# More products of a constant tile on TensorE in the first attention units of a fused attention and gated feed-forward kernel

## The chip, the cores and the metric

One NeuronCore of a Trainium2 chip runs the whole program. The metric is the device time of one execution in microseconds (us), as the median of several runs. Runs of one kernel spread by about 0.3% here.

## The reference

Three stages are computed one after the other, all in float32 at the interface. The weights of the second stage arrive as 64-bit floats.

```python
def _attn_ref(q, k, v, n_sink, window):       # q, k, v: (4, 8, 768, 64)
    scores = scale * np.matmul(q, k.transpose(0, 1, 3, 2))
    keep = is_sink | in_window                # 4 sink columns, window of 128
    scores = np.where(keep, scores, -1000000000.0)
    a = np.exp(scores - max); a = a / (sum + 1e-09)
    return np.matmul(a, v)

def _moe_ref(x, w_gate, w_val, w_out):        # x: (3072, 512), d_ff 1536
    gate = 1.0 / (1.0 + np.exp(-(x @ w_gate)))
    return gate * (x @ w_val) @ w_out

def _moe2_ref(x, phi, w1, w2):                # 8 experts of 4 slots, soft routing
    d = softmax over tokens of (x @ phi); slot_input = d.T @ x
    slot_out[e] = np.maximum(slot_input[e] @ w1[e], 0.0) @ w2[e]
    return softmax over slots of (x @ phi) @ slot_out
```

## The kernel before

The tokens of the four batches are cut into eight half-sequences of 384 tokens. Each has four pairs of heads, and each pair has three units of 128 queries; so a half-sequence is units 0 to 11, the next 12 to 23, and so on.

A unit u of attention goes through pieces, which a list puts in a fixed order. `stage_a(u)` ("scores") multiplies queries and keys of the two heads on TensorE (PE, L301; each head fills 64 of the 128 rows), reduces the masked scores on VectorE (DVE, L305), takes the exponential on ScalarE (ACT, L322) and queues the normalisation (DVE L326 and L327, GpSimd or POOL L328). `stage_b(u)` ("transposes") transposes the probabilities on PE (L362 or L368) and copies them out of PSUM on ACT (L363, L375). It stands two units behind the scores. `stage_c(n)` ("values") multiplies by the values for a whole pair of heads (PE L393, L396) and copies the result into the rows `xh` that the next stage reads. It stands behind the transposes of the pair's third unit.

The feed-forward stage (`gemm1`, L633; `gemm2`, L671) works on a half-sequence in steps of two blocks of 128 hidden columns. A gate or value product of the first half-sequence is four full float32 products of 384 columns, one for each pair of heads (d = 0 to 3), summed in a PSUM tile of the tag `gv`. It can take its first three products before the last pair's values are there. The weights come from 64-bit floats by a chain of ACT (L514, L515), DVE (L518, L519, L522) and POOL (L526); DVE's three instructions of one weight block are called a conversion here.

Program order is: the pieces of attention until the first half-sequence's values are complete, and then the feed-forward steps with the other pieces between them. A scheduler that simulates a timeline then chooses each engine's final order, so steps of the feed-forward stage can stand among the attention pieces. PSUM tiles come from rings in program order: `gv` has three banks, `ys` (scores and second products) has three, `pt` and `xt` one each.

`warm_pe(k)` takes a `gv` tile and issues k products of a constant bf16 tile of zeros, `blank` (128 x 128 against 128 x 512, L267). They are called blanks here. Nobody reads their result. The blanks stay in program order on PE among the instructions that the scheduler places. In the kernel before, 12 stand at the beginning (L1009), and one ahead of the scores piece of each of the units 0 to 5.

Of the kernel before, what the change touches and what calls it, by code (L numbers as in the profile page):

```python
# [36 lines left out]
def fused_kernel(ctx, tc, qT, kA, kB, vB, vS, wg, wv, wo, phi, w1, w2, n_sink, window, out):  # L37
# [10 lines left out]
    def ps(tag, bufs, dt=F32):  # L48
        return psum.tile([128, 512], dt, name=tag, tag=tag, bufs=bufs)
# [213 lines left out]
    def warm_pe(k):  # L263

        t = ps("gv", 3)
        for _ in range(k):
            tc.keep_in_program_order(pe.matmul(t, blank[:, 0:128], blank, start=True, stop=True, skip_group_check=True))  # L267
# [154 lines left out]
    def attn_piece():  # L422
        if not pieces:
            return False
        f, u = pieces.popleft()
        emitted[0] += 1
        if f is stage_a and u < 6:
            warm_pe(1)
        f(u)
        if f is stage_c:  # L430
            c_done[0] += 1
            done_half[0] = c_done[0] // 4
        return True
# [184 lines left out]
    def gemm1(si, c, kind):  # L618
# [3 lines left out]
        if si == h_first[h] and c == 0 and kind == "g":  # L622
            while xs_n[0] <= x_order.index(h):
                while not x_can():
                    assert attn_piece()
                    tick()
                x_split()
# [378 lines left out]
    load_pair(0)  # L1006
    load_pair(1)
    pool.memset(blank, 0.0)
    warm_pe(12)  # L1009
    warm = per.tile([1, 1], F32, name="warm")  # L1010
    dve.memset(warm, 0.0)
    act.activation(out=warm, in_=warm, func=ACTF.Exp)
    with tc.tile_pool(name="setup", bufs=1) as cp:
        setup_masks(cp)
        attn_piece()
        attn_piece()
        for _ in range(3):
            w_load()
        sp.dma_start(out=phi_sb, in_=phi.rearrange("(k p) s -> p k s", p=128))
        setup_rest(cp)  # L1020
# [123 lines left out]
```

## Time and profile before

| | |
|---|---|
| median of 3 runs | 934.28 us (931.99 to 934.65) |
| the profiled execution | 932.42 us, span 930.6 us |
| PE busy | 893.3 us (96%) |
| DVE busy | 576.4 us (62%) |
| POOL, ACT busy | 475.6 us, 375.1 us |
| mean granted clock of PE | 0.971 |
| HBM | 116.62 MB read, 15.73 MB written |

The profile is of one execution. Busy time of PE counts from a product's start to a modelled end, so neighbouring products overlap in it. The granted clock is a share of 2.4 GHz: 1.00 is 2.4 GHz, 0.50 is 1.2 GHz. A half-sequence's attention runs alone until some 68 us; from there PE works on the feed-forward stage with attention between, and from some 740 us on the last half-sequence, the routing and the experts follow.

### The profile page before, as it was taken

To read this page: it belongs to the slowest core of one execution; us is meant where nothing else is said; L and a number is where in the kernel's file an instruction comes from. 1 tells how busy PE (TensorE), PEld (TensorE's weight loads), DVE (VectorE), ACT (ScalarE), POOL (GpSimd) and SP (SyncE) were. 2 spreads that over 40 slices of the span, in tenths; PEclk is the share of its full clock that TensorE was granted. 3 is DMA by queue.
4 is the path that set the end of the run, shared out by engine and by line. 5 is a ranking of instruction groups with operands and counts; after the bars stand their busy time and mean duration, and the time that the engine had idled before them with its cause. 6 is when DMAs were issued, how large, how long until landed. Compare 5 with 4: busy or idle time off the path is not lost. (4 is left out here: it accounts for less than half of the span.)

```text
span 930.6 us, 15349 instructions
## 1 busy us (share of the span) xinstructions
PE 893.3 (96%) x5277; PEld 712.4 (77%) x5277; DVE 576.4 (62%) x1620; ACT 375.1 (40%) x1000; POOL 475.6 (51%) x428
## 2 busy tenths in 40 slices
PE   8789999999999999999999999999999999899894
PEld 4445555567799999988889899898999997798453
DVE  7986769776566758765676667765555434444522
ACT  6775656443343344343443333443323223241221
POOL 4743436572566675665685746564545422684000
PEclk7789999999999999999999999999999999999897
DMA  7975557541222342322232323331222169656997
GB/s 234 309 249 170 206 163 263 172 112 46 80 72 76 92 112 64 89 80 83 64 113 73 98 77 103 83 87 51 72 57 68 47 235 387 225 157 193 306 332 237
DMA packets 80356, 133.41 MB, mean 143 GB/s; under 512 B 6800, under 2 KB 38544, under 8 KB 80272
## 3 DMA queue, kind: packets, MB, share of 16 engines
q1 hardware_dynamic: 80272, 132.37, 45.3%
q8 instruction: 43, 0.70, 0.3%
q14 instruction: 41, 0.34, 0.1%
HBM read 116.62 MB, written 15.73 MB: 142 GB/s over the span
## 5 line engine op out<-in xcount | busy, mean ns | idle before, releaser
L633 PE MATMUL gv<-xh,whv 128*128 128x384 f32 x432 | 151.0, 379 | 2.5 <-ACT whv L190 2.5
L633 PE MATMUL gv<-xh,whg 128*128 128x384 f32 x432 | 153.0, 383 | 0.0
L650 POOL TENSOR_TENSOR gl<-th,gh 128x384 fp32r<-128x384 f32 x84 | 88.6, 1055 | 117.1 <-DVE gh L192 95.9
L671 PE MATMUL ys<-who,gh 128*128 128x512 f32 x324 | 138.7, 455 | 1.5 <-DVE gh L192 1.5
L676 DVE SCALAR_TENSOR_TENSOR ysb<-ys,ysb 128x512 f32<-128x512 f32 x138 | 93.3, 685 | 38.9 <-PE ys L671 38.0
L633 PE MATMUL gv<-xh,wlv 128*128 128x384 f32 x336 | 114.6, 341 | 0.7 <-POOL wlv L496 0.7
L633 PE MATMUL gv<-xl,whv 128*128 128x384 f32 x336 | 114.1, 340 | 0.0
L633 PE MATMUL gv<-xl,whg 128*128 128x384 f32 x336 | 114.1, 340 | 0.0
L633 PE MATMUL gv<-xh,wlg 128*128 128x384 f32 x336 | 113.5, 338 | 0.0
L671 PE MATMUL ys<-wlo,gh 128*128 128x512 f32 x252 | 99.4, 395 | 0.0
L671 PE MATMUL ys<-who,gl 128*128 128x512 f32 x252 | 98.6, 396 | 0.0
L322 ACT ACTIVATE PC<-P,nb 128x132 f32<-128x132 f32 (+1 forms) x152 | 60.1, 396 | 91.2 <-DVE P L316 74.2
L328 POOL TENSOR_TENSOR PC<-PC,sm 128x264 f32<-128x264 f32 (+1 forms) x76 | 51.5, 677 | 88.5 <-DVE sm L297 61.4
L633 PEld LDWEIGHTS gv<-xh,whv 128*128 128x128 f32 x432 | 81.6, 190 | 18.3 <-issue 4.3
L633 PEld LDWEIGHTS gv<-xh,whg 128*128 128x128 f32 x432 | 81.4, 190 | 15.6 <-issue 4.9
L646 DVE SCALAR_TENSOR_TENSOR th<-th,gv 128x384 f32<-128x384 f32 x84 | 46.3, 551 | 69.7 <-PE gv L633 58.0
L496 POOL TENSOR_TENSOR wlv<-wraw,whv 128x512 fp32r<-128x512 f32 x48 | 63.6, 1326 | 47.6 <-ACT whv L190 39.2
L671 PEld LDWEIGHTS ys<-who,gh 128*128 128x128 f32 x324 | 59.7, 188 | 29.4 <-issue 18.2
L305 DVE CUSTOM_DVE_ANT_0 P<-ys,mask 128x260 f32<-128x260 f32 (+1 forms) x152 | 57.2, 392 | 39.3 <-PE ys L301 38.9
L496 POOL TENSOR_TENSOR wlg<-wraw,whg 128x512 fp32r<-128x512 f32 x48 | 62.9, 1310 | 31.8 <-ACT whg L190 28.7
L637 ACT ACTIVATE th<-gv 128x384 f32<-128x384 f32 x96 | 46.8, 488 | 80.2 <-PE gv L633 79.2
L496 POOL TENSOR_TENSOR wlo<-wraw,who 128x512 fp32r<-128x512 f32 x48 | 61.6, 1299 | 9.0 <-ACT who L190 7.0
(210 smaller groups left out, 1788.7 us busy)
## 6 DMA issues: line engine op xcount, KB each, us to landing
ew<-in_w_dram SPq DMA_DIRECT2D x32, 1024.0 KB, 12.0
wraw<-wsg SPq DMA_DIRECT2D x48, 256.0 KB, 2.7
wraw<-wsv SPq DMA_DIRECT2D x48, 256.0 KB, 2.6
wraw<-wso SPq DMA_DIRECT2D x48, 256.0 KB, 2.6
wbits<-in_wg_dram SPq DMA_DIRECT2D x12, 512.0 KB, 4.6
wbits<-in_wv_dram SPq DMA_DIRECT2D x12, 512.0 KB, 4.9
wbits<-in_wo_dram SPq DMA_DIRECT2D x12, 512.0 KB, 4.6
out_dram<-ew SPq DMA_DIRECT2D x8, 768.0 KB, 6.8
```

The source lines that it names most:

```text
L305: dve.tensor_tensor_reduce(out=P[:, h, 0:w], in0=S[:, 0:w], in1=mask[:, MOFF[mt]:MOFF[mt] + w], scale=-0.125, scalar=3.0e38, op0=ALU.add, ...
L322: act.activation(out=dst[:, h], in_=src[:, h], func=ACTF.Exp, scale=-1.0, bias=nb[:, h:h + 1], accum_out=sm2[:, h, 0:1])
L328: pool.tensor_tensor(dst, dst, sm.unsqueeze(2).to_broadcast([128, 2, src.shape[2]]), op=ALU.mult)
L496: pool.tensor_tensor(lo, r, hi.bitcast(F32), op=ALU.subtract)
L633: pe.matmul(acc_ps[:, 0:384], wt[:, 128 * d:128 * d + 128], xt[:, d, :], start=(k == 0), stop=(k == 4 * len(seq) - 1))
L637: act.activation(out=th, in_=acc_ps[:, 0:384], func=ACTF.Tanh, scale=0.5)
L646: dve.scalar_tensor_tensor(gr, th, 1.0, acc_ps[:, 0:384], op0=ALU.add, op1=ALU.mult)
L650: pool.tensor_tensor(gl, gr, gh.bitcast(F32), op=ALU.subtract)
L671: pe.matmul(yp, a[:, 128 * i:128 * i + 128], w, start=(k == 0), stop=(k == len(seq) * len(ns) - 1))
L676: dve.scalar_tensor_tensor(ysb[h][:, i, :], yp, 0.5, ysb[h][:, i, :], op0=ALU.mult, op1=ALU.add)
```

## The change

The blanks at the beginning are 24 in place of 12. The blanks among the pieces are three ahead of every scores piece and every transposes piece of the units 0 to 14, in place of one ahead of the scores pieces of the units 0 to 5. That is 114 in place of 18.

```diff
         f, u = pieces.popleft()
         emitted[0] += 1
-        if f is stage_a and u < 6:
-            warm_pe(1)
+
+        if f is not stage_c and u < 15:
+            warm_pe(3)
         f(u)
...
     pool.memset(blank, 0.0)
-    warm_pe(12)
+    warm_pe(24)
```

The edit moves other instructions too, since the scheduler places them anew. Lines behind L427 are one higher in the changed kernel (L633 is L634 there, L518, L519 and L522 are L519, L520 and L523).

On PE, around the transpose of pair 1's sink columns (`Tb`), the kernel before has this (`gv_724`, `gv_742`, `gv_799` are the first gate, the first value and the second gate product of the first half-sequence):

```order
L301 MATMUL ys_631<-rk_432,rq_431 128x260
L362 MATMUL pt_476<-ident_61,PW_391 128x128 x4
L372 MATMUL xt_483<-identr_62,Tb_128 128x128
L633 MATMUL gv_724<-xh_420,whg_348 128x384
L633 MATMUL gv_742<-xh_420,whv_373 128x384
L633 MATMUL gv_799<-xh_420,whg_794 128x384
L301 MATMUL ys_632<-rk_432,rq_431 128x260
```

and the changed kernel this, with the repeated rows of each three blanks left out:

```order
L267 MATMUL gv_460<-blank_137 128x512
...
L267 MATMUL gv_469<-blank_137 128x512
...
L267 MATMUL gv_496<-blank_137 128x512
...
L372 MATMUL xt_539<-identr_62,Tb_128 128x128
...
L267 MATMUL gv_507<-blank_137 128x512
...
L267 MATMUL gv_528<-blank_137 128x512
...
L362 MATMUL pt_532<-ident_61,PW_427 128x128 x4
```

The three product steps of d = 0 are gone from this place, and fifteen blanks stand around the transpose. The steps of d = 1 and d = 2 of the same three products, which stand behind pairs 2 and 3 in the kernel before, are gone from their places likewise.

On PE, where the first half-sequence's values end (L396 of pair 3) and the first gate product gets its fourth step, the kernel before has:

```order
L396 MATMUL xt_695<-ttb_130,vs_332 128x256
L362 MATMUL pt_731<-ident_61,PW_626 128x128 x4
L301 MATMUL ys_870<-rk_527,rq_526 128x260
L301 MATMUL ys_871<-rk_527,rq_526 128x260
L633 MATMUL gv_724<-xh_420,whg_348 128x384
L633 MATMUL gv_742<-xh_420,whv_373 128x384
L633 MATMUL gv_799<-xh_420,whg_794 128x384
L301 MATMUL ys_963<-rk_622,rq_621 128x260
```

and the changed kernel (`gv_832`, `gv_854` and `gv_915` are the same three products):

```order
L634 MATMUL gv_832<-xh_456,whg_376 128x384 x3
...
L396 MATMUL xt_803<-ttb_130,vs_356 128x256
...
L301 MATMUL ys_991<-rk_595,rq_594 128x260
L634 MATMUL gv_832<-xh_456,whg_376 128x384
...
L267 MATMUL gv_839<-blank_137 128x512
L634 MATMUL gv_854<-xh_456,whv_403 128x384 x4
...
L267 MATMUL gv_891<-blank_137 128x512
L634 MATMUL gv_915<-xh_456,whg_910 128x384 x4
...
L267 MATMUL gv_950<-blank_137 128x512
```

Of the nine steps that the kernel before has done by then, the changed one has the first product's three, just ahead; the other two products come whole behind it, and nine blanks stand between.

On DVE, between the score reductions (L305) of unit 14 and unit 15, the kernel before has:

```order
L305 ISA PW_678,nb_679<-ys_684,mask_125 128x260
L305 ISA nb_679 128x1
L522 SCALAR_TENSOR_TENSOR wA_1073<-wbits_1045,wA_1073 128x512
L326 TENSOR_REDUCE sm_681<-sm2_680 128x2
L305 ISA PW_756,nb_757<-ys_761,mask_125 128x260
```

and the changed kernel:

```order
L305 ISA PW_786,nb_787<-ys_792,mask_125 128x260
...
L519 TENSOR_SCALAR wA_1231<-wA_1231 128x512
L520 TENSOR_SCALAR wA_1231<-wA_1231 128x512
L523 SCALAR_TENSOR_TENSOR wA_1231<-wbits_1200,wA_1231 128x512
L326 TENSOR_REDUCE sm_789<-sm2_788 128x2
...
L519 TENSOR_SCALAR wA_1289<-wA_1289 128x512
L340 CAST Ta_127<-PC_717 128x12x4
L520 TENSOR_SCALAR wA_1289<-wA_1289 128x512
L341 TENSOR_TENSOR Ta_127<-PC_717,Ta_127 128x12x4
L523 SCALAR_TENSOR_TENSOR wA_1289<-wbits_1251,wA_1289 128x512
L305 ISA PW_868,nb_869<-ys_873,mask_125 128x260
```

Two whole conversions stand there now in place of the last instruction of one. Ahead of unit 14 twelve conversions and two instructions of the thirteenth stand in the kernel before, and thirteen in the changed one.

## Rows read from the trace of the kernel before

**Rows 1.** Busy time by stretch; the columns are named in the first row.
```profile
core 0: us, PE busy (x) PEld busy (x) DVE busy (x) ACT busy (x) POOL busy (x), PEclk, DMA share, GB/s
8.83:60.27 51.44, 40.78 (x185) 24.27 (x185) 46.04 (x153) 38.56 (x114) 30.63 (x26) 0.73 0.86 284
...
68.02:140.00 71.98, 71.98 (x302) 40.28 (x300) 50.24 (x133) 42.06 (x109) 29.14 (x24) 1.00 0.55 180
...
200.00:740.00 540.00, 540.00 (x3300) 477.20 (x3301) 341.17 (x973) 205.10 (x571) 310.77 (x280) 1.00 0.27 78
740.00:930.60 190.60, 166.74 (x1169) 129.21 (x1167) 77.08 (x169) 50.41 (x105) 61.58 (x52) 0.94 0.78 256
```

**Rows 2.** Waits of PE, 66 to 760 us: total, times, longest.
```profile
PE ys L301 <- DVE nb L305: 0.5, 1, 0.5
```

**Rows 3.** Timeline of PE at the start: start, duration, what.
```profile
1.31 5.66 PE L267 MATMUL gv<-blank 128*128 128x512 bf16 x13 [1.31 <-POOL blank L1008]
6.90 0.49 PE L301 MATMUL ys<-rk,rq 64*128 64x128 f32 x4
```

**Rows 4.** Timeline of PE, one-pass products of 512 columns in a stream.
```profile
739.28 0.39 PE L671 MATMUL ys<-who,gh 128*128 128x512 f32 x1
739.51 0.39 PE L671 MATMUL ys<-wlo,gh 128*128 128x512 f32 x1
739.74 0.40 PE L671 MATMUL ys<-who,gl 128*128 128x512 f32 x1
```

**Rows 5.** Busy time by stretch of one clock level, first half-sequence.
```profile
10.20:20.40 10.20, 9.69 (x33) 6.49 (x34) 7.64 (x44) 8.99 (x29) 4.49 (x4) 0.50 0.75 238
20.40:23.80 3.40, 2.28 (x13) 1.29 (x11) 3.40 (x12) 2.74 (x9) 2.67 (x3) 1.00 0.83 270
23.80:34.00 10.20, 7.19 (x35) 4.77 (x35) 10.06 (x38) 7.98 (x25) 7.18 (x7) 0.50 0.99 329
...
37.50:40.90 3.40, 3.40 (x6) 1.46 (x5) 3.37 (x6) 2.23 (x5) 2.62 (x4) 0.50 0.88 281
...
47.70:51.10 3.40, 3.40 (x6) 1.19 (x5) 2.06 (x9) 3.31 (x8) 0.99 (x2) 0.50 0.87 298
51.10:61.40 10.30, 7.67 (x52) 4.59 (x51) 9.21 (x21) 6.41 (x18) 5.84 (x5) 1.00 0.79 274
```

**Rows 6.** Timeline of PE, steps of the gate and value products.
```profile
37.31 1.45 PE L633 MATMUL gv<-xh,whg 128*128 128x384 f32 x2
...
67.27 0.91 PE L633 MATMUL gv<-xh,whg 128*128 128x384 f32 x2
...
70.59 2.79 PE L633 MATMUL gv<-xh,whv 128*128 128x384 f32 x8
```

**Rows 7.** Waits of DVE, 8.83 to 60.27 us.
```profile
DVE PW L305 <- PE ys L301: 2.1, 2, 1.6
DVE PW L305 <- PE pt L362: 1.0, 1, 1.0
DVE wA L518 <- ACT wA L514: 1.0, 1, 1.0
DVE P L305 <- PE ys L301: 0.5, 1, 0.5
```

**Rows 8.** Timeline of DVE: first reductions of units 0, 14, 16, and a mask step.
```profile
8.83 0.28 DVE L305 CUSTOM_DVE_ANT_0 P<-ys,mask 128x128 f32<-128x128 f32 x1
...
9.25 0.56 DVE L99 TENSOR_SCALAR mask<-mask 128x780 f32<-128x780 f32 x1
...
60.27 0.41 DVE L305 CUSTOM_DVE_ANT_0 PW<-ys,mask 128x260 f32<-128x260 f32 x1
...
66.15 0.43 DVE L305 CUSTOM_DVE_ANT_0 PW<-ys,mask 128x260 f32<-128x260 f32 x1
```

**Rows 9.** Groups of DVE instructions, 8.83 to 60.27 us: the conversions.
```profile
L518 DVE TENSOR_SCALAR wA<-wA 128x512 f32<-128x512 f32 x13 | 10.1, 774 | 1.0 <-ACT wA L514 1.0
L519 DVE TENSOR_SCALAR wA<-wA 128x512 int32<-128x512 int32 x13 | 9.9, 760 | 0.3
L522 DVE SCALAR_TENSOR_TENSOR wA<-wbits,wA 128x512 int32<-128x512 int32 x12 | 9.7, 808 | 0.2
```

## The prediction, made before the changed kernel ran

> **What bounds the kernel now.** I read the table of busy time by stretch first [rows 1]. It shows three regimes. From 68 us to 740 us TensorE (PE) is busy without a gap at a granted clock of 1.00, and from 66 to 760 us the list of waits holds a single one of PE, 0.5 us long [rows 2]. Whatever PE work is still undone when that stretch begins therefore moves the end. After 740 us PE is busy 166.74 of 190.6 us; I take that tail to move as a whole, since it starts from PE's last products. Before 68 us, attention of the first half-sequence fills the time: PE is busy 40.78 of 51.44 us between 8.83 and 60.27, DVE 46.04 of 51.44, at a mean PE clock of 0.73.
>
> Then I read that early part by clock level [rows 5]. The clock is 0.50 (1.2 GHz) in four stretches between 10.2 and 51.1 us, 27.2 us in all. In the first of these PE was busy 9.69 of 10.20 us, mostly with scores, which fill 64 of 128 rows. The clock there follows what PE works on, not only whether it works: between 51.1 and 61.4 us it stayed at 1.00 with PE busy 7.67 of 10.30 us. The 13 products at the start also ran at the low level although the clock column reads 1.00 there: 5.66 us for 13 is 435 ns each [rows 3], while a 512-column one-pass product late in the kernel follows its predecessor by 0.23 to 0.24 us [rows 4]. I price a blank product at 0.235 us at 2.4 GHz and 0.435 at 1.2 GHz. The Trainium skill (TensorE: Matmul & The Clock Gate, "Back-to-back issue gap") gives 216 ns for an isolated 512-column product at full clock; by it the blanks behind the first half would cost 0.2 us less, and no row here shows a blank in a stream at that level.
>
> Last I read DVE. It is idle 5.4 us between its first score reduction at 8.83 and that of unit 14 at 60.27 [rows 1, 8]; 3.6 us of that are waits for PE and 1.0 for ACT [rows 7]. Its work there is 46.04 us, of which some 30 are conversions of 64-bit weights [rows 9]. So the first half is DVE's stretch, with PE second.
>
> **The change part by part.** There are 24 blanks at the start and 30 pieces with three each, 114 in place of 18.
>
> The first 24: 13 run as before, to 6.97 us, and by then the stream has raised the clock, since the scores behind it run at the higher level (two of 128 columns begin at 6.90 and are through in 0.49 us [rows 3]). Ahead of those scores stand 27 now (24 and the first piece's three), so 14 more, 14 x 0.235 = 3.3 us: the first scores begin near 10.2 us. DVE read them at 8.83 before. In the new DVE order the 0.56 us mask step of L99 [rows 8] and four smaller steps stand ahead of that read, so most of the delay is covered. I charge 0.4 us; without that cover it is 1.4.
>
> The blanks inside the first half: by PE's order 105 of the 114 stand ahead of the first complete gate product, 27 of them ahead of the first scores, so 78 fall into the attention stretch, 78 x 0.235 = 18.3 us. What room is there? PE idles 10.66 us between 8.83 and 60.27 [rows 1]. In the four slow stretches it is busy 9.69 + 7.19 + 3.40 + 3.40 = 23.7 us [rows 5]; at 2.4 GHz half of that, 11.8 us, comes back. And nine one-column-block steps of the gate and value products, which filled holes there (the first three at 37.31 [rows 6]), leave the stretch: 9 x 0.70 = 6.3, with 0.70 from eight records in 2.79 us [rows 6]. Room 28.8 us, need 18.3: it fits if the clock stays up, and it does not if it falls: at 1.2 GHz the same blanks are 34 us and the 11.8 do not come back. I take the upper level for nearly all of it, because a stream of blanks alone raised the clock at the start.
>
> What that gives DVE: its waits for PE, 3.6 us, can go. Against that stand 0.8 us (by the new DVE order one third of a weight conversion more is done ahead of unit 14, a third of 774 + 760 + 808 ns [rows 9]), the 0.4 from above, and waits of the new order: scores now stand behind up to nine blanks and wait for one of three PSUM banks that DVE frees, so a late score is followed by a late blank. The trace has no row for that; it is between nothing and the 3.6 us that DVE waited for PE. I take 0.9. Unit 14: 8.83 + 46.04 + 0.8 + (5.4 - 3.6 + 0.4 + 0.9) = 58.8 against 60.27, so 1.5 us earlier. The ends are 55.7 (DVE never waits), 4.6 us earlier, and 2 us later.
>
> From unit 14 to unit 16: before, DVE came to unit 16's first reduction at 66.15, 5.9 us later, with less than one conversion between [rows 8]. Now two whole conversions, 2 x 2.34 = 4.7 us, stand between units 14 and 15; with the four score reductions, the norm and the two small steps it is 7.1 us: 1.2 us later. The scores that need those banks stand on PE ahead of the first full-depth step, so PE waits for it. With unit 14 earlier by 1.5, the first full-depth step ends 0.3 us earlier in sum.
>
> What is late next: the nine product steps that ran in holes. By the new order three of them stand just before that point and six do not run before it: the two other accumulators are now requested after the blanks' tiles in the same ring of three banks. That is 6 x 0.70 = 4.2 us of PE work carried into the stretch without gaps. The last nine blanks (units 12 to 14, transposes) stand in that stretch too: 9 x 0.235 = 2.1 us. Together 6.3 us, with nothing to hide it [rows 1, 2].
>
> Later PE order is the same from about 200 us on. The SP queue moves its weight loads and a value load ahead of two of the q/k loads; these are needed units later, so I cost that at nothing; the 1.0 us wait for ACT [rows 7] is what such loads cost at their worst before.
>
> Sum: -0.3 + 6.3 = +6.0 us. The profiled execution took 932.42 us (930.6 span plus 1.8 around it), so 938.4 by it; the median of the runs is 934.28, 1.86 above it, so 940.3 by that. I forecast 940.
>
> **A rule weighed.** The stretch from 68 to 140 us shows PE busy throughout, yet weight loads are busy only 40.28 of 71.98 us, against 477.20 of 540 between 200 and 740 [rows 1]. The Trainium skill (Trainium Kernel Development and Optimization, "Performance Expectations") says that busy time of matmuls is a bad measure of how near PE is to its limit and that the share of weight loads is a good one. By it PE would still have room until 140 us and part of the 6.3 us would vanish; with half of it gone the sum is that of the first rival below. The rows speak against: the eight records in 2.79 us are four full fp32 products of 384 columns with no gap between [rows 6], and such products hold the array long for each weight load.
>
> **Rivals.**
> No change: the carried work is half absorbed between 68 and 200 us, where DVE is the other busy engine. Then -0.3 + 3.1 = +2.8, 937.1; or DVE never waits, -4.6 + 1.2 + 6.3 = +2.9, 937.2. For it: PE's busy time has modelled ends. Against: only one wait of PE is listed.
> Faster: attention was held by the slow clock, DVE loses all 5.4 us of its idle time, and PE absorbs all the carried work after 68 us. -4.6 + 1.2 = -3.4, 930.9. It decides only if the stretch after 68 us has 6 us of room.
> Much slower: the clock does not stay up, because blanks are split into threes with scores and waits between. PE's load between 8.83 and 60.27 at 2.4 GHz would be 51.4 - 28.8 - 0.9 (four old blanks) + 18.3 = 40.0 us; with half of it at 1.2 GHz it is 60 us, PE becomes the bound and unit 14 comes 8.6 us later instead of 1.5 earlier: 934.3 + 8.6 + 1.2 + 6.3 = 950. It decides from the point where over 29% of that work runs slow (40.0 x 1.29 = 51.4).
> That the blanks do nothing for the clock is the same case: the old rate, 27.2 slow of 51.4 us, is about the half that I priced.
>
> **How the numbers follow.** Forecast (937.5 to 945): 0.54. No change: 0.23. Faster: 0.10. Slow clock: 0.13. A measurement of this kernel can tell about 0.3%, 2.8 us, from no change. Faster 0.10; within 0.3% 0.22 (nearly all of the no-change case); slower 0.68. The range leaves out the faster case and the far part of the slow-clock case: 934 to 948; the likeliest case's own is 937.5 to 945.
>
> **What would show it.** Right: granted clock near 1.00 from about 7 to 66 us with at most one or two short drops; blanks 0.235 us apart; DVE waits for PE under 2 us before unit 14; nine blanks and the second and third accumulators' first steps behind the first complete gate product; that product ending at 67 to 68 us; PE without gaps behind it and every later landmark about 6 us later. Wrong: that product ending before 62 us, PE gaps between 68 and 200 us, or long stretches at 0.50 with blanks 0.43 us apart.

## The result, and the profile after

The changed kernel takes 943.58 us (median of 4 runs, 942.95 to 944.04), the kernel before 934.46 (4 runs, 931.99 to 935.05). The ratio is 1.0112 with a 95% interval of 1.0089 to 1.0136: slower by 9.1 us. Forecast was 940, with a range of 934 to 948. The profiled execution took 944.04 us (span 942.2), so the two profiles shown are 11.6 us apart, of which 10.4 are there by 740 us.

**Stretches.** Busy time by stretch of the changed kernel, with the columns of [rows 1]:

```profile
8.83:63.58 54.75, 49.59 (x250) 26.43 (x248) 48.78 (x154) 39.99 (x115) 29.60 (x26) 0.84 0.84 276
10.73:63.58 52.85, 47.69 (x240) 25.62 (x239) 47.04 (x149) 39.99 (x115) 29.60 (x26) 0.84 0.83 271
15.80:22.60 6.80, 6.50 (x18) 3.17 (x18) 6.42 (x21) 4.98 (x16) 4.24 (x4) 0.50 0.86 273
22.60:29.50 6.90, 5.95 (x34) 3.55 (x32) 6.37 (x33) 6.25 (x18) 5.26 (x6) 0.99 0.97 321
29.50:39.70 10.20, 9.56 (x42) 5.61 (x42) 8.31 (x29) 7.76 (x29) 5.72 (x6) 0.50 0.88 295
39.70:63.58 23.88, 21.48 (x136) 11.53 (x133) 21.34 (x52) 16.21 (x41) 12.74 (x11) 1.00 0.73 236
72.12:140.00 67.88, 67.88 (x284) 37.09 (x283) 41.62 (x111) 38.49 (x99) 26.24 (x23) 1.00 0.48 159
200.00:740.00 540.00, 539.80 (x3303) 475.36 (x3301) 345.59 (x983) 206.17 (x577) 314.72 (x283) 1.00 0.28 80
```

Two stretches of the first half are left at 0.50, 17.0 us together, where [rows 5] show four of 27.2. PE's mean clock up to unit 14 rose from 0.73 to 0.84, and its busy share from 79% to 91%. The wait list of PE from 66 to 760 us again holds a single wait, so the long stretch has no gap here either:

```profile
PE ys L672 <- DVE nb L305: 1.0, 1, 1.0
```

**Start.** Timeline of PE (start, duration, what), which answers to [rows 3]:

```profile
1.31 8.08 PE L267 MATMUL gv<-blank 128*128 128x512 bf16 x27 [1.31 <-POOL blank L1009]
9.32 0.49 PE L301 MATMUL ys<-rk,rq 64*128 64x128 f32 x4
9.75 0.82 PE L267 MATMUL gv<-blank 128*128 128x512 bf16 x3
```

The first scores come at 9.32, not at 10.2, and three blanks are through in 0.82 us: at the upper level the blanks are about 0.22 us apart.

**Landmarks.** Timeline of DVE: the first reductions of units 0, 14 and 16 [rows 8], and of two later units, 54 and 95:

```profile
10.73 0.28 DVE L305 CUSTOM_DVE_ANT_0 P<-ys,mask 128x128 f32<-128x128 f32 x1
...
63.58 0.42 DVE L305 CUSTOM_DVE_ANT_0 PW<-ys,mask 128x260 f32<-128x260 f32 x1
...
70.24 0.43 DVE L305 CUSTOM_DVE_ANT_0 PW<-ys,mask 128x260 f32<-128x260 f32 x1 [0.66 <-PE pt L362]
...
355.45 0.29 DVE L305 CUSTOM_DVE_ANT_0 P<-ys,mask 128x128 f32<-128x128 f32 x1 [1.67 <-PE ys L301]
...
733.04 0.43 DVE L305 CUSTOM_DVE_ANT_0 P<-ys,mask 128x260 f32<-128x260 f32 x1 [1.76 <-PE ys L301]
```

The same two late units in the kernel before:

```profile
345.01 0.29 DVE L305 CUSTOM_DVE_ANT_0 P<-ys,mask 128x128 f32<-128x128 f32 x1 [1.47 <-PE ys L301]
...
722.60 0.43 DVE L305 CUSTOM_DVE_ANT_0 P<-ys,mask 128x260 f32<-128x260 f32 x1 [1.76 <-PE ys L301]
```

Unit 0 is 1.9 us late, unit 14 3.3, unit 16 4.1, units 54 and 95 both 10.4. So 4.1 us are lost while attention runs alone, 6.3 us between unit 16 and unit 54, and nothing from there to 740.

**The first complete gate product.** Timeline of PE:

```profile
64.06 0.70 PE L301 MATMUL ys<-rk,rq 64*128 64x260 f32 x2 [1.25 <-DVE nb L305]
64.70 2.20 PE L634 MATMUL gv<-xh,whg 128*128 128x384 f32 x6
...
69.60 0.60 PE L362 MATMUL pt<-ident,PW 128*128 128x128 f32 x4
...
71.37 0.91 PE L634 MATMUL gv<-xh,whg 128*128 128x384 f32 x2
72.12 0.81 PE L267 MATMUL gv<-blank 128*128 128x512 bf16 x3
72.76 2.74 PE L634 MATMUL gv<-xh,whv 128*128 128x384 f32 x8
...
76.62 0.81 PE L267 MATMUL gv<-blank 128*128 128x512 bf16 x3
77.27 2.74 PE L634 MATMUL gv<-xh,whg 128*128 128x384 f32 x8
...
80.53 0.82 PE L267 MATMUL gv<-blank 128*128 128x512 bf16 x3
```

The first product has its three early steps just ahead (six records at 64.70), the next two come whole behind it (eight records each), and nine blanks stand between, as the order said.

**DVE.** Its waits from 8.83 to 63.58 us (total, times, longest) and its conversions, which answer to [rows 7, 9]:

```profile
DVE wA L519 <- POOL who L527: 1.5, 1, 1.5
DVE PW L305 <- PE pt L362: 1.2, 1, 1.2
DVE wA L519 <- ACT wA L515: 1.0, 3, 0.4
DVE xh L192 <- PE xt L396: 0.6, 1, 0.6
DVE P L305 <- PE ys L301: 0.5, 1, 0.5
DVE PW L305 <- PE ys L301: 0.4, 1, 0.4
```

```profile
L519 DVE TENSOR_SCALAR wA<-wA 128x512 f32<-128x512 f32 x13 | 11.7, 899 | 2.5 <-POOL who L527 1.5 <-ACT wA L515 1.0
L523 DVE SCALAR_TENSOR_TENSOR wA<-wbits,wA 128x512 int32<-128x512 int32 x13 | 10.6, 814 | 0.1
L520 DVE TENSOR_SCALAR wA<-wA 128x512 int32<-128x512 int32 x13 | 9.4, 720 | 0.3
```

The waits for PE shrank only from 3.6 to 2.7 us, and waits in the conversion chain (for POOL and ACT) grew from 1.0 to 2.5.

### The profile page after: what moved, and what is told of

Same layout as the page of the kernel before. It is cut to its first block, busy times and chain, and to the rows that moved or that the text cites. A ratio compares the mean times of both kernels' runs of the same rounds, so it can differ in the third digit from the quotient of the medians.

```text
span 942.2 us, 15531 instructions
## 1 busy us (share of the span) xinstructions
PE 910.1 (97%) x5373; PEld 715.8 (76%) x5373; DVE 578.8 (61%) x1620; ACT 375.5 (40%) x1000; POOL 473.0 (50%) x428
## 4 chain that ended last, share of the span: by engine, by line
## 5 line engine op out<-in xcount | busy, mean ns | idle before, releaser
L634 PE MATMUL gv<-xh,whg 128*128 128x384 f32 x432 | 151.3, 379 | 0.0
L634 PE MATMUL gv<-xh,whv 128*128 128x384 f32 x432 | 150.5, 376 | 0.5 <-ACT whv L190 0.5
L634 PE MATMUL gv<-xh,wlv 128*128 128x384 f32 x336 | 114.3, 340 | 0.7 <-POOL wlv L497 0.7
L634 PE MATMUL gv<-xl,whg 128*128 128x384 f32 x336 | 114.6, 341 | 0.0
L634 PE MATMUL gv<-xh,wlg 128*128 128x384 f32 x336 | 113.8, 339 | 0.1
L634 PE MATMUL gv<-xl,whv 128*128 128x384 f32 x336 | 113.8, 339 | 0.0
L634 PEld LDWEIGHTS gv<-xh,whg 128*128 128x128 f32 x432 | 80.4, 188 | 15.0 <-issue 4.2
L634 PEld LDWEIGHTS gv<-xh,whv 128*128 128x128 f32 x432 | 80.5, 189 | 13.9 <-issue 3.0
L305 DVE CUSTOM_DVE_ANT_0 P<-ys,mask 128x260 f32<-128x260 f32 (+1 forms) x152 | 56.9, 393 | 39.3 <-PE ys L301 39.0
## 6 DMA issues: line engine op xcount, KB each, us to landing
ew<-in_w_dram SPq DMA_DIRECT2D x32, 1024.0 KB, 12.2
```

The costliest lines, as they stand in the source:

```text
L305: dve.tensor_tensor_reduce(out=P[:, h, 0:w], in0=S[:, 0:w], in1=mask[:, MOFF[mt]:MOFF[mt] + w], scale=-0.125, scalar=3.0e38, op0=ALU.add, ...
L634: pe.matmul(acc_ps[:, 0:384], wt[:, 128 * d:128 * d + 128], xt[:, d, :], start=(k == 0), stop=(k == 4 * len(seq) - 1))
```

## The experiments

Twelve kernels ran. The table has the time against the kernel before on the same chip. Its other columns come from each profile, from 1.31 us to the first reduction of unit 54: PE's idle time; the blanks (for each the time from its start to the next product's start, or to its own end where that comes first); and the rest, which is PE's own products with what the low clock adds to them. The three add up to the column "unit 54" less 1.31. A profile is of one execution: those of e2 and e5 are 2.9 us faster than their kernels' medians. Up to four blanks have no record in those of e1, e2, e4 and e12, which moves a column by less than 1 us.

| kernel | median us | ratio (95%) | unit 14 | unit 54 | blanks | idle | rest |
|---|---|---|---|---|---|---|---|
| before | 932.67 to 934.46 | | 60.27 | 345.01 | 7.9 | 12.1 | 323.6 |
| changed | 943.58 | 1.0112 (1.0089 to 1.0136) | 63.58 | 355.45 | 29.5 | 7.0 | 317.6 |
| e1 units 0 to 5 only | 935.72 | 1.0027 (1.0016 to 1.0039) | 62.40 | 346.81 | 18.3 | 8.7 | 318.5 |
| e2 no nine late blanks | 942.75 | 1.0109 (1.0089 to 1.0129) | 62.00 | 352.53 | 27.1 | 7.4 | 316.7 |
| e3 64 columns | 942.91 | 1.0102 (1.0086 to 1.0119) | 63.60 | 355.64 | 13.2 | 10.5 | 330.7 |
| e4 one in place of three | 939.52 | 1.0076 (1.0055 to 1.0098) | 55.30 | 350.79 | 16.1 | 12.8 | 320.6 |
| e5 one blank in all | 932.14 | 0.9990 (0.9972 to 1.0007) | 58.05 | 341.72 | 0.6 | 13.2 | 326.6 |
| e6 12 at the start, no others | 929.25 | 0.9950 (0.9930 to 0.9969) | 54.95 | 340.19 | 4.5 | 12.4 | 322.0 |
| e7 24 at the start, then as before | 933.29 | 0.9997 (0.9986 to 1.0008) | 62.34 | 344.32 | 9.2 | 10.9 | 322.9 |
| e8 12 at the start, then as changed | 939.23 | 1.0056 (1.0038 to 1.0073) | 57.88 | 350.45 | 26.0 | 9.1 | 314.0 |
| e9 one PSUM tile for all blanks | 947.48 | 1.0157 (1.0131 to 1.0182) | 65.70 | 359.62 | 28.7 | 9.4 | 320.3 |
| e10 256 columns | 937.49 | 1.0049 (1.0034 to 1.0065) | 57.17 | 349.37 | 20.5 | 8.0 | 319.6 |
| e11 before, 12 more late | 934.10 | 1.0011 (0.9998 to 1.0024) | 60.16 | 345.72 | 10.5 | 12.2 | 321.7 |
| e12 before, 48 more late | 945.22 | 1.0126 (1.0104 to 1.0147) | 59.51 | 349.61 | 11.2 | 12.9 | 324.2 |

Only the first 24 of e12's 48 stand ahead of unit 54.

What the low clock adds can be estimated and taken out of the rest: half of PE's busy time on its own products in the stretches at 0.50. That is 12.8 us before, 5.9 in the changed kernel, 17.5 in e3, 10.5 in e6, 2.3 in e8, and 14.6 in e5 (the last section says why its clock column shows almost none of it). What is left is 309 to 314 us in all fourteen kernels. So PE's own work to unit 54 hardly changes, and the times differ by blanks, idle time and the low clock.

**e1, blanks in the first six units only**

```diff
-        if f is not stage_c and u < 15:
+        if f is not stage_c and u < 6:
```

> Three blanks ahead of the scores and transposes pieces of units 0 to 5 only, 24 at the start: 60 blanks. In the new order all nine early product steps stand ahead of the first complete gate product again and no blank behind it; the conversions on VectorE are as in the changed kernel up to unit 12, and 13 stand ahead of unit 14, 14 ahead of unit 16 (before 13 and a third, changed 15). Backlog theory (six steps and nine late blanks, 6.3 us, added behind the first complete gate product): every later landmark moves by no more than that product does, so the 6.3 us are gone. Conversion theory (attention is late by the conversions that the new order puts ahead of unit 16): product late by about 0.5 x 2.3 = 1 us, total 935.5. Blank-time theory (the blanks' own run time on TensorE delays attention): 33 of the 78 blanks of the stretch are left, so unit 14 late by 0.42 x 3.3 = 1.4 us, total 936. If the backlog theory is wrong: over 940.

Measured 935.72, 2.5 us over before, and unit 16 and unit 54 late by 1.5 and 1.8: nothing is added behind unit 16. That fits the backlog theory, and 935.5 or 936 doesn't part the other two. (In the table its blanks are 10.4 us more than before, idle time 3.4 and the rest 5.1 less.)

**e2, the changed kernel without its nine late blanks**

```diff
-        if f is not stage_c and u < 15:
+        if (f is stage_a and u < 15) or (f not in (stage_a, stage_c) and u < 12):
```

> As the changed kernel, without the blanks ahead of the transposes of units 12 to 14, nine of 114. These nine stood behind the first complete gate product; without them the ring of three banks frees earlier in program order too, and the new order has all nine early product steps ahead of that product. Conversions as in the changed kernel: 13 ahead of unit 14, 15 ahead of unit 16. Backlog theory: first complete gate product as in the changed kernel (72.1 us, 4.1 later than before), nothing added behind it: every later landmark +4, total 938.5. Without the backlog theory (only blank time counts): the nine blanks are worth 2.1 us, total 941.5.

A miss: 942.75, not 938.5; the other theory's 941.5 is nearer. The timeline of PE shows where the early steps went:

```profile
62.48 0.70 PE L301 MATMUL ys<-rk,rq 64*128 64x260 f32 x2 [1.25 <-DVE nb L305]
63.12 2.20 PE L634 MATMUL gv<-xh,whg 128*128 128x384 f32 x6
65.25 0.70 PE L301 MATMUL ys<-rk,rq 64*128 64x260 f32 x2
65.88 1.56 PE L634 MATMUL gv<-xh,whv 128*128 128x384 f32 x4
...
69.14 2.10 PE L634 MATMUL gv<-xh,whg 128*128 128x384 f32 x6
...
73.78 0.91 PE L634 MATMUL gv<-xh,whg 128*128 128x384 f32 x2
```

and DVE's first reduction of unit 16:

```profile
73.25 0.43 DVE L305 CUSTOM_DVE_ANT_0 PW<-ys,mask 128x260 f32<-128x260 f32 x1 [3.36 <-PE pt L362]
```

All nine steps (18 records) stand ahead of the first complete gate product again, but in no hole: PE has no gap from 62.48 until behind the last of them, and DVE waits 3.36 us for the transpose behind them. Unit 16 is 7.1 us late in place of 4.1, and little is added later. Which side of that product a step stands on decides only where the lateness shows. This led to the budget theory: until some 350 us the time is PE's products, plus blanks, plus idle time, plus the low clock's loss.

**e3, narrow blanks**

```diff
-            tc.keep_in_program_order(pe.matmul(t, blank[:, 0:128], blank, start=True, ...
+            tc.keep_in_program_order(pe.matmul(t[:, 0:w], blank[:, 0:128], blank[:, 0:w], start=True, ...
```

(w is 64 among the pieces and 512 at the start.)

> As the changed kernel, but the blanks among the pieces are 64 columns wide in place of 512 (the 24 at the start stay); 13 conversions ahead of unit 14 and 15 ahead of unit 16, as in the changed kernel; early product steps as in the changed kernel. Blank-time theory: unit 14's first reduction falls back to 60 us or earlier (63.58 changed, 60.27 before), first complete gate product near 68, then 4.2 for six steps and 0.5 for nine narrow blanks: 939. Conversion theory: unit 14 near 63 and the product near 72 in spite of the narrow blanks, total 943. The granted clock tells besides whether narrow blanks hold it as wide ones do (0.84 mean from 10.7 to 63.6 us in the changed kernel, 0.73 before).

Unit 14 at 63.60 and 942.91 us are the conversion theory's numbers, but not by its way. The stretch up to unit 14:

```profile
10.73:63.60 52.87, 44.34 (x241) 28.57 (x242) 44.75 (x150) 38.95 (x116) 29.99 (x26) 0.58 0.82 266
```

DVE was idle 8.1 us of it (5.8 in the changed kernel), and the clock fell to 0.58, below the 0.73 of the kernel before. Blanks fell by 16.3 us, the rest rose by 13.1 and idle time by 3.5: the same total. So the wide blanks do hold the clock better than narrow ones, and they cost what that gives back.

**e4, one in place of three**

```diff
-            warm_pe(3)
+            warm_pe(1)
```

> As the changed kernel, but one blank ahead of every such piece in place of three (24 at the start stay): 54 in all. By the new order the six steps stay behind the first complete gate product and three late blanks with them: backlog 4.2 + 0.7 = 4.9. Ahead of unit 14 stand only 11 conversions, ahead of unit 16 13 (before 13 and a third and 13 and two thirds; changed 13 and 15). Conversion theory: unit 14 at about 56 to 58, the product at 67 to 68, total 934.5 - 0.5 + 4.9 = 939. Blank-time theory: a third of the delay, 1.4, total 934.5 + 1.4 + 4.9 = 941.

Unit 14 comes at 55.30, earlier than the conversion theory's 56 to 58, and the total of 939.5 is that theory's 939, but not by its way. Unit 16 is 3.9 us early and unit 54 5.8 late: 9.7 us appear between them where 4.9 were expected. PE idles 2.9 us there (0.5 before), and the clock is at 0.50 from 170.6 to 174.0, which costs 1.7. When DVE reaches unit 14 does not set the end. The mean clock from 10.70 to 55.30 is 0.85, no lower than the 0.84 of the changed kernel: with one blank per piece it was held as well as with three.

**e5 and e6, none among the pieces**

```diff
-        if f is not stage_c and u < 15:
-            warm_pe(3)
         f(u)
...
-    warm_pe(24)
+    warm_pe(1)      # e5; 12 in e6
```

> One blank in all, at the start, none among the pieces. VectorE's conversions stand as before (13, 12 and 12 parts ahead of unit 14, 14, 13 and 13 ahead of unit 16), and the nine early product steps too. Budget theory (new, from the first four runs: until some 300 us TensorE's time is its own work, some 312 us, plus the blanks' time, plus its idle time, plus what the low clock costs, and the sum of the last three was 32.8 us before, 42.4 in the changed kernel): blanks fall from 7.9 to about 0.4 us; if nothing else moves, 7.5 us faster, 926; if blanks are what holds the clock, the loss by the low clock rises from 12.8 towards 20 and the total stays within 2 us of 933. Order theory (the time is set by when VectorE reaches units 14 and 16): no change, 933 to 934, and unit 14's first reduction at 60 to 61 us.

> 12 blanks at the start, none among the pieces (before has six there). Ahead of unit 14 stand 11 conversions, ahead of unit 16 13 (before 12.7 and 13.3). Budget theory: 6 x 0.235 = 1.4 us less of blanks, and less or more by what the six do for the clock: 930 to 934. Order theory: unit 14 at 56 to 57 us, unit 16 at 65, total 932 to 933.

e5 cannot be told from before (0.9990, runs from 929.3 to 936.2): 7.3 us of blanks less, rest and idle 4.1 more in its profile. The budget's 926 is out; its other case (within 2 us of 933) and the order theory's total are not told apart, though unit 14 at 58.05 is earlier than the order theory's 60 to 61. e6 is the fastest of all, 929.25, with the whole interval of its ratio at least 0.3% below 1. Against before, its blanks are some 3.5 us less, idle 0.3 more and the rest 1.6 less. Its first reduction of unit 54, at 340.19, comes 4.8 us earlier than that of before. The order theory's 932 to 933 is missed by 3, the budget's 930 to 934 by 0.8. Without the six blanks among its pieces, and with the order that the scheduler then finds, the kernel before is 0.5% faster.

**e7 and e8, the two halves of the edit**

```diff
-        if f is not stage_c and u < 15:
-            warm_pe(3)
+        if f is stage_a and u < 6:
+            warm_pe(1)      # e7: 24 at the start stay
...
-    warm_pe(24)
+    warm_pe(12)             # e8: three per piece stay
```

> 24 blanks at the start, among the pieces as before (one ahead of the scores of units 0 to 5). Budget theory: 12 x 0.235 = 2.8 us more of TensorE time ahead of the first scores (at 9.3 us against 6.9), paid back only as far as TensorE's idle time falls: 934 to 936.5. Order theory: 14 conversions ahead of unit 14 and 14.7 ahead of unit 16, one and a third and one more than before: unit 14 at 62 to 63 us, total +2 to +3, 936. Cover theory of the prediction (VectorE's other work hides the later start): 933.5 to 934.

> 12 blanks at the start, three ahead of every scores and transposes piece of units 0 to 14 as in the changed kernel. Six steps and nine late blanks stay behind the first complete gate product. Budget theory: 2.6 us of blanks less than the changed kernel, 940 to 941. Cover theory: as the changed kernel, 942.5 to 943.5.

24 at the start alone make no difference (933.29 against 933.75), though unit 14 is 2.1 us late. That is nearest the cover theory's 933.5 to 934; the budget's 934 to 936.5 is missed by 0.7, the order theory's 936 by 2.7. The pieces' blanks alone make 5.5 us of the 9.1: 939.23, near the budget's 940 to 941 and 3.3 below the cover theory's range. The halves don't add up: 12 more at the start cost nothing beside the old pieces, and 3.6 us (9.1 less 5.5) beside the new ones, where the rest is 3.6 us higher (317.6 against 314.0). e8 was at 0.50 for less time, a loss of 2.3 us against 5.9. Why the longer start brings the low clock back is open.

**e9, one bank for all blanks**

```diff
-        t = ps("gv", 3)
+        if not blank_t:
+            blank_t.append(ps("gv", 3))
+        t = blank_t[0]
```

> All 114 blanks of the changed kernel, but all write one PSUM tile of the tag gv that is taken once, so that two of the three banks are free for the gate and value products from the start. By the new order the first two accumulators' three early steps each stand among the attention pieces again (six steps), and the third product whole behind the first complete gate product, with nine late blanks. 15 conversions stand ahead of unit 14 and of unit 16. Carried-steps theory (of the prediction: the six steps are lost because the blanks hold the ring): the three steps of one more accumulator and more come back, total 940 to 941. Budget theory (TensorE's time until some 300 us is its own work plus blanks, idle and the low clock's loss, wherever a step stands): blanks take their 29.5 us as in the changed kernel, idle plus low clock at 11 to 13 us as there: 942 to 945.

947.48, the slowest of all. Giving six early steps their banks back did not bring their 4.2 us back. It is also above the budget's 942 to 945, by 2.5 us: idle time and the low clock's loss are 15.6 us in place of 11 to 13. Between units 16 and 54 PE idles 3.6 us (1.3 in the changed kernel), and the clock is at 0.50 from 199.2 to 202.6, which costs 1.6. Why the new order waits there is open.

**e10, half as wide**

```diff
-            warm_pe(3)
+            warm_pe(3, 256)
```

> As the changed kernel, but the 90 blanks among the pieces are 256 columns wide in place of 512 (64 in the narrow kernel); the 24 at the start stay 512 wide. 11 conversions stand ahead of unit 14, 13 ahead of unit 16. Budget theory: blanks 8.1 us for the first 27 and some 10 us for the others, 18 in sum. If the clock holds as with wide blanks (loss by the low clock 6 us, idle 8): sum 32, 933 to 935. If it falls as with narrow ones (loss 17.5, idle 10.5): sum 46, over 945. Order theory: unit 14 at 56 us, and 4.2 for six steps and 1 for nine late blanks: 936 to 938.

937.49, between the two cases of the budget: blanks 9.0 us less than in the changed kernel, idle and rest 3.0 more. The half-width blanks hold the clock less well: its mean is 0.78 from 10.59 to 57.17 us, between the 0.84 of the changed kernel and the 0.73 before, and the loss is 6.7 us against 5.9. The order theory's 936 to 938 fits too, though unit 14 at 57.17 is followed by unit 54 4.4 us late.

**e11 and e12, more blanks where nothing is idle**

```diff
         if f is stage_a and u < 6:
             warm_pe(1)
+        if f is stage_a and u == 40:                  # e11
+        if f is stage_a and u in (40, 52, 64, 76):    # e12
+            warm_pe(12)
```

> The kernel before with twelve more blanks in one place, ahead of the scores piece of unit 40, in the stretch where TensorE has no gap and the clock is at its upper level. The order up to there is that of before. Budget theory: nothing covers them, so every landmark behind them moves by 12 x 0.22 = 2.6 us, total 936. If the stretch has hidden room (the weighed rule of the prediction): 0 to 1 us.

Inconclusive: twelve blanks take 2.7 us, and unit 54 moves by 0.7, the median by 1.1. The timeline of PE has them without a gap:

```profile
233.06 2.76 PE L267 MATMUL gv<-blank 128*128 128x512 bf16 x12
```

The rest is 1.9 us lower. The scheduler had also reordered 50 us around them, and scores, value and gate products took less time from start to start there. So the order may be worth a microsecond or two by itself; e12 bears on that.

> The kernel before with four times twelve more blanks, ahead of the scores pieces of units 40, 52, 64 and 76, all in the stretch in which TensorE has no gap and runs at the upper clock level. The run with twelve showed 2.7 us of blanks and a shift of only 0.7 to 1.1 us, with the order of the stretch around them changed. Budget theory (uncovered blanks cost their time; what twelve gave back was the luck of one new order, about 2 us): 48 x 0.22 = 10.6 us of blanks, total +8.5 to +11, 942 to 944. Hidden-room theory (some 60% of added work disappears wherever it is put): +3 to +4.5, 936 to 938.

945.22, above the budget's 942 to 944 and far from hidden room's 936 to 938. First reductions of units 16, 51, 54, 72, 80 and 95 in e12:

```profile
66.78 0.43 DVE L305 CUSTOM_DVE_ANT_0 PW<-ys,mask 128x260 f32<-128x260 f32 x1 [1.01 <-PE pt L362]
...
322.79 0.29 DVE L305 CUSTOM_DVE_ANT_0 P<-ys,mask 128x128 f32<-128x128 f32 x1
...
349.61 0.29 DVE L305 CUSTOM_DVE_ANT_0 P<-ys,mask 128x128 f32<-128x128 f32 x1 [1.68 <-PE ys L301]
...
502.97 0.29 DVE L305 CUSTOM_DVE_ANT_0 P<-ys,mask 128x128 f32<-128x128 f32 x1 [1.68 <-PE ys L301]
...
566.31 0.42 DVE L305 CUSTOM_DVE_ANT_0 P<-ys,mask 128x260 f32<-128x260 f32 x1
...
735.00 0.43 DVE L305 CUSTOM_DVE_ANT_0 P<-ys,mask 128x260 f32<-128x260 f32 x1 [1.76 <-PE ys L301]
```

and of units 51, 72 and 80 in the kernel before:

```profile
321.35 0.29 DVE L305 CUSTOM_DVE_ANT_0 P<-ys,mask 128x128 f32<-128x128 f32 x1
...
493.74 0.29 DVE L305 CUSTOM_DVE_ANT_0 P<-ys,mask 128x128 f32<-128x128 f32 x1 [1.68 <-PE ys L301]
...
553.92 0.41 DVE L305 CUSTOM_DVE_ANT_0 P<-ys,mask 128x260 f32<-128x260 f32 x1
```

Unit 16 is late by 0.6, unit 95 by 12.4: 48 blanks and the new order added 11.8 us. The four groups of twelve differ. The second stands at 328 us, the fourth at 531: from unit 51 to 54, and from unit 72 to 80, the lateness grows by 3.2 us each (1.4 to 4.6, and 9.2 to 12.4), somewhat more than twelve spacings of 0.216. The first adds 0.8 only, as in e11, whose changed order from 219 to 269 us e12 shares. The third adds 4.6 with another order, and not by blanks alone: PE idles 2 us between 424 and 439, where the kernel before has no gap, and the clock is at 0.50 from 435.1 to 438.5. In the second and the fourth only a few products change places. So where the order hardly changes, a blank in the stretch without gaps costs its whole time; the hidden-room theory falls for that stretch, and what e11's twelve gave back is put down to the order.

## Why the prediction came out as it did

The sign and the range held, and the forecast of +6 was 3.1 us short of the medians, 5.6 of the two profiles. Of the prediction's own signs, blanks some 0.22 us apart, the order around the first complete gate product and a long stretch without gaps came. The clock near 1.00, waits of DVE for PE under 2 us (2.7 measured), that product's end at 67 to 68 us (72.1) and landmarks about 6 us late (10.4) did not.

- *The backlog of 6.3 us.* Units 54 and 95 are late by 10.4, unit 16 by 4.1: 6.3, the predicted number, of which 5.6 are busy time of PE and 0.8 its idle time. The order is the one shown above, but that the number agrees to a tenth is luck: the same count gives 4.7, 4.9 and 4.2 us in e3, e4 and e9, and 7.5, 9.7 and 10.3 were measured. What did not hold is the cause given for its first part, that six steps were lost to the ring of banks: e2 and e9 gave steps their places back and stayed slow. In e2 the same nine steps made unit 16 later. In the kernel before they had run in PE's holes; with blanks in the holes, a free bank brought nothing back.
- *"Room 28.8 us, need 18.3: it fits."* This is the step that failed, and in it the 11.8 us that were to come back from the clock. The prediction took the upper level for nearly all of the first half; 17.0 us stayed at 0.50, and to unit 54 the clock's loss fell from 12.8 us to 5.9, by 6.9 only. (Of the 12.8, 1.7 belong to a fifth stretch at 0.50 in the kernel before, 61.40 to 64.80, behind unit 14.) The blanks' time rose by 21.6 us to unit 54 (29.5 less 7.9); idle time gave back 5.1 and the rest, which the clock's part is in, 6.0. But for rounding, that leaves the 10.4 by which unit 54 is late. The 6.3 us of the steps were room in the first half alone: the prediction itself charged 4.2 of them again behind it.
- *Unit 14 at 58.8.* It came at 63.58, 3.3 late in place of 1.5 early. The terms: the start 1.9 (0.4 charged), DVE's work from its first reduction on 1.0 (0.8 charged), its idle time 0.4 more (5.8 of 52.85 us against 5.4 of 51.44) where 2.7 less was expected. The cover of the late start was there (DVE was busy 1.74 of the 1.90 us), but unit 14 was not spared as much later: from 8.83 on DVE was busy 48.78 us against 46.04. Of these 2.7, 2.0 are conversions (31.7 against 29.7): a third of one more, and longer ones (899 against 774 ns for the first instruction). The waits for PE did not go, and waits for POOL and ACT joined them.
- *Unit 14 to 16.* 6.66 us against 5.88: 0.8 more, 1.2 predicted.
- *First scores near 10.2.* At 9.32: most of the 27 products ran at the upper level (8.08 us in all), and blanks there are 0.22 us apart, not 0.235. The twelve of e11 say the same: less one duration of 0.38, 2.76 us are 0.216 for each of eleven spacings. The Trainium skill (TensorE: Matmul & The Clock Gate, "Back-to-back issue gap") gives 216 ns for an isolated product of 512 columns and about 131 for one in a stream. The trace has 216 in a stream, and the measurement decides.
- *The rule weighed.* The Trainium skill (Trainium Kernel Development and Optimization, "Performance Expectations") calls busy time of matmuls a poor measure. The rows' side held: all 6.3 us of the backlog are there at unit 54, although weight loads were busy only 37.09 of 67.88 us between 72 and 140. e12's groups at 328 and 531 us stand where weight loads are busy 477.20 of 540 us [rows 1], so they test the stretch without gaps, not the place where the rule saw room.
- *The rivals.* "Much slower", a clock that doesn't stay up, happened in part: 17.0 us low against 27.2 up to unit 14. It needed over 29% of 40.0 us of work at the low level; PE was busy 16.1 us there, which is 8.0 us of work at 2.4 GHz, or 20%. "No change" and "faster" asked for carried work to vanish after 68 us, and it did not.

What the runs put in place of a chain through unit 14 is a budget of PE. e4 and e10 have unit 14 early by 5.0 and 3.1 us and end late; e7 has it 2.1 us late and ends even. That the three add up is arithmetic. What the runs add is that the rest, less the low clock's loss, stays within 309 to 314 us; that PE time put into the stretch without gaps costs its length where the order hardly changes (e12); and that blanks made narrow cost as much in clock and waits as they save (e3). The budget is good to some 2.5 us, since a new order moves the rest (e11) and can bring waits and a low clock into the long stretch (e4, e9, e12). What makes the clock fall in one kernel and not in another stays open.

## What to carry to other kernels

When an engine runs without a gap for most of a kernel, price filler work on it by the whole span: its time, less the idle time that really goes, less what the clock gives back, all read from the stage that it fills. Holes that other useful work already uses are not room. Try the start alone first: twelve products there and none later was the best of the 14 kernels, 929.25 us, 0.5% below the kernel before.

## What was not expected of the hardware

The clock column does not show a cold start. With one blank in all (e5) it reads 1.00 from 7.70 to 58.05 us, yet four transposes at 34.32 take 1.06 us. In the changed kernel four such transposes take 0.60 to 0.66 where the column reads 1.00, as at 69.60 above, and 1.11 at 33.53, where it reads 0.50. In e5:

```profile
7.70:58.05 50.35, 42.10 (x182) 24.94 (x181) 48.51 (x160) 38.96 (x115) 29.54 (x26) 1.00 0.91 299
```

```profile
34.32 1.06 PE L362 MATMUL pt<-ident,PW 128*128 128x128 f32 x4
...
39.62 0.70 PE L301 MATMUL ys<-rk,rq 64*128 64x260 f32 x2
```

In the changed kernel:

```profile
33.53 1.11 PE L362 MATMUL pt<-ident,PW 128*128 128x128 f32 x4
```

By 39.62 the scores of e5 run at full rate. Its trace has the first entry of the clock at 35.6 us; in the changed kernel the first stands at 5.6, where the blanks' spacing falls from 0.43 us to 0.22. PE is busy 26.4 us ahead of that entry in e5, so the cold start cost it half of that on its own products, 12.9 us, and another stretch at 0.50 cost 1.7: together 14.6, where the kernel before loses 12.8. So with 17 blanks fewer, 7.3 us of them, e5 lost only 1.8 us more to the clock than the kernel before.

Narrow blanks were no better for the clock than none: 0.58 from 10.73 to 63.60 us with over 70 of 64 columns, 0.73 in the stretch from 8.83 us of [rows 1] with four of 512, and 0.71 from 8.00 to 54.95 in e6 with none.
